# A fused attention and token-mixing kernel on one core: a new order of all units, with other evicting engines, PSUM banks and load order

## The chip, the cores and the metric

The kernel runs on one core of one Trainium2 chip. The metric is the device time of one execution in microseconds (us); smaller is better. Three timed runs of the kernel before gave 109.33, 109.36 and 109.76, median 109.36.

## What is computed

There are two parts, one behind the other. B = 4 batches, H = 8 heads, S = 768 positions, D = 64 values per head, 8 blocks of 96 positions.

```python
P = sort_net                                   # 8x8 per batch and head
for _ in range(5):                             # Sinkhorn: rows, then columns
    P = exp(P - max(P, -1)); P /= sum(P, -1); P /= sum(P, -2)
k_sorted = einsum('bhij,bhjcd->bhicd', P, k_blocks)      # mix whole blocks
v_sorted = einsum('bhij,bhjcd->bhicd', P, v_blocks)
attn = softmax(q_blocks @ k_sorted^T / 8)      # inside each block of 96
x = (attn @ v_sorted)  -> (B, S, 512)          # heads side by side
W = (x @ w_q) @ (x @ w_k)^T / 8
out = relu(W @ x) @ w_out
```

The inputs q, k, v are float32 in DRAM and are cast to bfloat16 by the load; the output is float32.

## The kernel before, in words

**Units.** The whole program is cut into small units, and a string, `ORDER` (L17 to L47), lists them one by one. The loop at L597 reads the list and calls one function per unit, which appends its instructions to its engine's queue. Nothing is scheduled by a tool: each engine runs its own units in just the order in which the string names them, and the framework adds a wait wherever a unit needs what another has written, or where a buffer or bank must first be read out. A unit's name is a kind, the batch and a number. An upper-case kind (other than R) is TensorE work, and the number after the colon is the PSUM bank that it writes. A lower-case kind is the eviction of that bank or other elementwise work, with the engine (A = ScalarE, called ACT; D = VectorE, called DVE; G = GpSimd, called POOL; S = SyncE, called SP) and the bank. So `K01:4 ... k01:A:4` is: unit K of batch 0, pair of heads 1, into banks 4 and 5; ACT evicts them.

The kinds, for a batch b:

- `lq`, `lk`, `lv` (L205): the load of q, k or v of one batch, 768 KB as bfloat16, issued by POOL; three buffers for each of the three inputs (`NIN`, L105). `lp` loads w_q and w_k, `lo` loads w_out.
- `i`, `c`, `a`, `p`, `B`, `u`, `n` (L158 to L241): constants; the Sinkhorn chain on DVE and ACT (`c00 a01 c01 ... a05 c05`); then its result laid out as mixing matrices `M` (unit `n`; for batch 0 on DVE from PSUM, for the others on POOL from the copy `PTR`).
- `Q`, `q` (L248): q transposed to `QT`. `K`, `k` (L269): k mixed by `M` and transposed in one step to `KT`, two banks.
- for batch 0 `Y`, `y`, `F`, `f` (L275 to L288): v mixed like k, then transposed back to `VT`. For the other batches `V`, `v` (L290): v mixed into the single buffer `Vs`, and six DMAs `R` on SP (L300), which move `Vs` row by row to `VT`.
- `S`, `e` (L304, L314): seven units of scores (S06, S16, ... are short) and their exponential on ACT, into `E`.
- `P`, `r`, `x` (L325 to L347): five units of attention times v (P04, P14, ... are short), reciprocal of the sums and product on DVE, into `X`.
- `T`, `t` (L350): X transposed to `XT`. `J`, `j`, `d`: the w_q and w_k product. `W`, `w`, `G`, `g`, `H`, `h`: the mixing, ending in `mixT` with the ReLU. `O`, `o`, `s`: six units of the last product, evicted to `ot` and stored by SP.
- `Z` (L243): filler. `Z09` multiplies a tile of zeros nine times and nobody reads it.

**Shared places.** PSUM has eight banks; a unit that writes a bank waits for the eviction of what stood there. `M`, `QT`, `KT`, `VT`, `E`, `X` have two buffers, `Vs` has one. POOL issues the loads one after the other between its `n` and `d` units, so a load stands behind whatever POOL waits for.

Of the kernel before, what the change touches and what calls it, by code (L numbers as in the profile page):

```python
# [14 lines left out]
NMIX = 2  # L15

ORDER = """  # L17
i02:D Z03:0 lq0 c00:D lk0 a01:A c01:D i00:G i03:G B01:0 p01:A a02:A p00:A:0 c02:D lq1 lv0 a03:A c03:D lv1
Z010:0 lk1 a04:A c04:D lp a05:A c05:D lk2 Q03:0 lq2 Q02:1 q03:A:0 Q01:2 B00:3 lo q01:D:2 q02:A:1 Q00:0 n03:D:3
lv2 n01:D:3 K03:1 n02:D:3 K01:4 q00:D:0 k03:A:1 lq3 K02:6 n00:D:3 k01:A:4 k02:D:6 S05:0 u00:A:3 S02:4 e05:A:0  # L20
S03:6 n10:G S04:2 e02:A:4 Q13:0 Q11:1 n11:G q13:D:0 e03:A:6 K00:4 q11:D:1 Q10:0 k00:A:4 S06:6 lk3 Q12:1
e06:A:6 S00:4 q12:D:1 q10:A:0 S01:6 e01:A:6 Y03:0 y03:A:0 e04:A:2 Y01:6 Y00:0 y01:D:6 y00:A:0 n20:G F03:3
Z09:2 f03:A:3 e00:A:4 F01:0 F00:1 f01:D:0 V12:2 f00:D:1 Y02:4 v12:A:2 P04:6 n21:G P01:0 r04:D:6 y02:A:4
x04:D:6 P00:2 R15:S r01:D:0 R14:S lv3 K13:4 r00:D:2 x01:D:0 K11:6 k13:A:4 k11:D:6 K10:0 S16:4 x00:D:2 e16:A:4
V11:6 V10:4 v11:A:6 k10:D:0 T00:3 n30:G F02:2 v10:A:4 t00:D:3 R13:S S11:0 f02:D:2 K12:6 R12:S e11:A:0 S10:4
n31:G k12:D:6 R10:S P02:2 e10:A:4 P03:0 R11:S r02:D:2 x02:D:2 S13:6 K20:4 e13:A:6 r03:D:0 T01:2 x03:D:0
k20:A:4 S14:6 t01:D:2 e14:A:6 T03:0 K22:3 t03:A:0 K23:1 k22:D:3 S15:6 T02:5 e15:A:6 k23:D:1 Q23:4 Q20:3
q23:A:4 Q22:6 t02:D:5 q20:D:3 q22:A:6 S12:0 P13:6 e12:A:0 J00:5 r13:D:6 x13:D:6 P10:3 j00:A:5 S24:0 d00:G
W00:5 r10:D:3 e24:A:0 P14:6 x10:D:3 J01:2 S20:0 j01:D:2 S25:3 e20:A:0 r14:D:6 w00:D:5 d01:G W01:2 x14:D:6
Q21:5 e25:A:3 P11:0 q21:D:5 S26:6 w01:D:2 T13:5 r11:D:0 e26:A:6 x11:D:0 V22:2 t13:A:5 V21:6 v22:A:2 P12:4  # L30
v21:D:6 V20:0 T10:2 R24:S r12:D:4 G00:3 v20:D:0 t10:A:2 R23:S K21:6 R22:S G01:3 k21:A:6 x12:D:4 R21:S Q31:0
g00:A:3 Q33:1 R20:S q31:D:0 H00:2 S21:4 R25:S q33:D:1 H02:6 h00:A:2 T11:0 h02:D:6 e21:A:4 T12:1 S22:2 t12:D:1
H01:6 t11:A:0 S23:4 h01:D:6 O00:1 e22:A:2 J11:0 o00:A:1 e23:A:4 K32:6 j11:D:0 K31:1 k32:D:6 d11:G J10:3
k31:D:1 K33:4 j10:A:3 K30:6 W10:3 d10:D k30:A:6 O02:0 k33:D:4 w10:A:3 W11:7 o02:A:0 S36:5 S35:3 w11:D:7 S32:1
e36:A:5 G10:7 e35:A:3 P22:5 e32:A:1 G11:7 r22:D:5 x22:D:5 V32:3 P23:0 v32:A:3 O05:2 g10:D:7 r23:D:0 x23:D:0
R35:S H11:6 o05:A:2 H10:4 R34:S Q30:3 h11:A:6 h10:D:4 T22:0 V30:1 q30:A:3 P24:6 t22:D:0 O11:5 v30:A:1 r24:D:6
x24:D:6 S30:3 o11:D:5 Q32:0 R31:S e30:A:3 P21:6 R30:S P20:1 q32:A:0 r21:D:6 V31:3 x21:D:6 T23:5 v31:A:3 O03:0
r20:D:1 t23:D:5 x20:D:1 S34:6 R32:S o03:A:0 S33:4 T21:3 R33:S e33:A:4 O04:0 t21:D:3 s01:S e34:A:6 S31:1
o04:D:0 H12:3 T20:5 e31:A:1 h12:D:3 O10:6 s02:S P32:0 o10:D:6 P33:2 r32:D:0 O01:4 s10:S r33:D:2 x32:D:0 O15:6
x33:D:2 P34:0 o15:A:6 O14:7 t20:D:5 P31:2 o01:D:4 o14:A:7 J20:5 r31:D:2 s00:S r34:D:0 x34:D:0 J21:4 s12:S  # L40
j20:A:5 x31:D:2 T32:7 d20:G j21:A:4 W20:0 T33:1 d21:G W21:6 w20:D:0 T31:2 t33:D:1 w21:A:6 G20:0 t31:D:2 P30:5
t32:D:7 G21:0 r30:D:5 x30:D:5 O12:7 g20:A:0 H21:0 o12:A:7 H20:2 H22:4 h21:D:0 h20:A:2 T30:6 O13:7 t30:D:6
O22:3 h22:D:4 o13:A:7 J30:2 s11:S o22:A:3 J31:7 j30:D:2 O21:6 d30:D j31:A:7 d31:D W30:7 W31:5 o21:A:6 O23:4
w31:D:5 w30:A:7 G30:7 o23:A:4 O24:6 s21:S G31:7 o24:A:6 O20:4 g30:A:7 H32:6 o20:D:4 H31:1 h32:A:6 O25:5
h31:D:1 s20:S H30:3 o25:A:5 O35:7 h30:D:3 s22:S O34:6 o35:D:7 O31:5 o34:A:6 s35:S O32:7 s34:S o31:A:5 O30:6
s31:S o32:A:7 O33:5 s32:S o30:A:6 s30:S o33:A:5 s33:S
"""  # L47


# [595 lines left out]
```

## Time and profile before

| what | value |
|---|---|
| median of 3 runs | 109.36 us |
| the profiled execution's own time | 109.27 us |
| its span (first to last instruction or transfer) | 107.4 us |
| TensorE (PE) matmul busy | 91.2 us, 85% |
| DVE busy | 72.3 us, 67% |
| ACT busy | 68.8 us, 64% |
| POOL busy | 28.4 us, 26% |
| loads, queue of POOL | 10.09 MB |
| stores and R transfers, queue of SP | 8.73 MB |

The span is 1.87 us shorter than the execution that it was taken from. "Busy" is time in which at least one instruction of the engine ran; for PE the ends of matmuls are modelled. PEld is the loading of weights, which goes on beside PE's matmuls. "PEclk" is the share of the full TensorE clock that was granted. In the lists of instructions a row has the start in us, the duration in us, the engine, the line, the operation, the tile written and the tiles read, a count (x24: so many merged into the row), and in brackets how long the engine stood idle before it and what ended that. Nearly all matmuls have line 143 and all copies line 147 (ACT) or 149 (DVE), since helpers issue them; they are told apart by their tiles.

### The profile page before, as it was taken

To read this page: it belongs to the slowest core of one execution; us is meant where nothing else is said; L and a number is where in the kernel's file an instruction comes from. 1 tells how busy PE (TensorE), PEld (TensorE's weight loads), DVE (VectorE), ACT (ScalarE), POOL (GpSimd) and SP (SyncE) were. 2 spreads that over 40 slices of the span, in tenths; PEclk is the share of its full clock that TensorE was granted. 3 is DMA by queue.
4 is the path that set the end of the run, shared out by engine and by line. 5 is a ranking of instruction groups with operands and counts; after the bars stand their busy time and mean duration, and the time that the engine had idled before them with its cause. 6 is when DMAs were issued, how large, how long until landed. Compare 5 with 4: busy or idle time off the path is not lost.

```text
span 107.4 us, 3466 instructions
## 1 busy us (share of the span) xinstructions
PE 91.2 (85%) x1475; PEld 61.4 (57%) x1486; DVE 72.3 (67%) x143; ACT 68.8 (64%) x99; POOL 28.4 (26%) x47
## 2 busy tenths in 40 slices
PE   5399477559889979599998999999999999999950
PEld 1135456453778868468985766785657755543410
DVE  3676963230479988399998858979899987219200
ACT  4404399796176998669789697989625174635550
POOL 6999122125897700011000100000001273000000
PEclk9999999985999999999999999999999999999999
DMA  0999999999999999999999400323974503145982
GB/s 3 100 198 205 203 205 205 203 204 205 186 204 215 228 233 243 205 205 203 207 209 263 85 6 0 101 55 96 359 279 166 240 0 148 50 198 206 362 310 98
DMA packets 18879, 19.04 MB, mean 177 GB/s; under 512 B 1840, under 2 KB 16944, under 8 KB 18864
## 3 DMA queue, kind: packets, MB, share of 16 engines
q0 software_dynamic: 14064, 10.09, 62.4%
q1 hardware_dynamic: 4800, 8.73, 23.5%
q8 instruction: 11, 0.18, 0.7%
q14 instruction: 4, 0.03, 0.1%
HBM read 20.19 MB, written 6.29 MB: 247 GB/s over the span
## 4 chain that ended last, share of the span: by engine, by line
PE 43%; DMA 24%; DVE 15%; POOL 8%; issue 4%; ACT 3%; DVEq 0%; SPq 0%; POOLq 0%; ACTq 0%
PE ps L143 43%; DMA Vn<-in_v_dram 17%; DMA VT<-Vs 7%; DVE X L344 6%; POOL M L239 2%; DVE mixT L410 2%; POOL Qn L215 2%; DVE Rall L339 1%; DVE Vs L149 1%; ACT Vs L147 1%; ACT E L315 1%; DVE ot L149 1%; POOL Kn L215 1%; DVE KT L149 1%; POOL Vn L215 1%
## 5 line engine op out<-in xcount | busy, mean ns | idle before, releaser
L315 ACT ACTIVATE E<-ps 96x960 bf16<-96x960 f32 (+1 forms) x28 | 24.4, 902 | 2.3 <-PE ps L143 2.1
L143 PE MATMUL ps<-wo,mixT 128*128 128x512 bf16 x86 | 22.4, 379 | 0.5
L344 DVE TENSOR_TENSOR X<-ps,Rall 96x896 bf16<-96x896 f32 (+1 forms) x20 | 19.8, 1000 | 0.4
L147 ACT COPY ot<-ps 128x512 f32<-128x512 f32 x18 | 10.6, 586 | 10.2 <-PE ps L143 10.1
L371 POOL COPY qD<-qkT 64x384 bf16<-64x384 bf16 x5 | 2.5, 503 | 43.9 <-ACT qkT L147 31.2
L143 PEld LDWEIGHTS <-mixT 128*128 128x128 bf16 x96 | 8.3, 98 | 8.6 <-issue 1.0
L143 PE MATMUL ps<-VT,E 96*128 96x65 bf16 x256 | 10.5, 193 | 1.3 <-DMA VT<-Vs 1.2
L149 DVE CAST KT<-ps 128x768 bf16<-128x768 f32 x10 | 9.4, 952 | 2.8 <-PE ps L143 2.8
L143 PEld LDWEIGHTS <-E 96*128 96x128 bf16 x256 | 9.3, 97 | 2.9 <-issue 1.7
L143 PE MATMUL ps<-fil 128*128 128x512 bf16 x21 | 9.1, 607 | 2.0 <-DVE fil L191 1.2
L143 PEld LDWEIGHTS <-KT 64*128 64x128 bf16 (+1 forms) x288 | 8.5, 98 | 4.1 <-issue 1.9
L147 ACT CAST KT<-ps 128x768 bf16<-128x768 f32 x10 | 7.9, 798 | 3.8 <-PE ps L143 3.7
L410 DVE TENSOR_SCALAR mixT<-ps 128x1024 bf16<-128x1024 f32 x8 | 9.8, 1222 | 0.5 <-PE ps L143 0.4
L147 ACT CAST Vs<-ps 128x1024 bf16<-128x1024 f32 x7 | 7.0, 1019 | 4.3 <-PE ps L143 3.8
L143 PE MATMUL ps<-QT,KT 64*128 64x96 bf16 x256 | 9.1, 204 | 0.5 <-ACT KT L147 0.5
L143 PE MATMUL ps<-idb,X 96*128 96x96 bf16 x128 | 8.0, 207 | 0.6 <-DVE X L344 0.6
L143 PE MATMUL ps<-idb,Qn 128*64 128x128 bf16 x192 | 7.5, 225 | 1.0 <-DMA Qn<-in_q_dram 0.9
L239 POOL TENSOR_TENSOR M<-PTR,m_p 128x512 bf16<-128x512 bf16 x6 | 7.8, 1310 | 1.3 <-PE ps L143 1.3
L143 PE MATMUL ps<-M,Kn 128*64 128x128 bf16 x192 | 7.2, 221 | 0.8 <-DVE X L344 0.4
L143 PEld LDWEIGHTS <-Qn 128*64 128x64 bf16 x192 | 6.2, 113 | 2.6 <-DMA Qn<-in_q_dram 1.9
L143 PEld LDWEIGHTS <-X 96*128 96x128 bf16 x128 | 6.2, 98 | 2.2 <-issue 0.6
L339 DVE RECIPROCAL Rall<-ps 96x14 f32<-96x14 f32 (+1 forms) x20 | 4.3, 223 | 4.7 <-PE ps L143 4.6
(79 smaller groups left out, 131.8 us busy)
## 6 DMA issues: line engine op xcount, KB each, us to landing
out_dram<-ot SPq DMA_DIRECT2D x9, 512.0 KB, 2.8
Qn<-in_q_dram POOLq DMA_DIRECT2D x4, 768.0 KB, 18.5
Kn<-in_k_dram POOLq DMA_DIRECT2D x4, 768.0 KB, 22.2
Vn<-in_v_dram POOLq DMA_DIRECT2D x4, 768.0 KB, 21.8
VT<-Vs SPq DMA_DIRECT2D x18, 132.0 KB, 5.8
out_dram<-ot SPq DMA_DIRECT2D x6, 256.0 KB, 2.0
wo<-in_moe_w_out_dram POOLq DMA_DIRECT2D x1, 512.0 KB, 25.1
wqk<-in_moe_w_q_dram POOLq DMA_DIRECT2D x1, 64.0 KB, 20.6
```

Source lines behind the costliest of these rows:

```text
L143: nc.tensor.matmul(o, w, x, is_transpose=t, start=start, stop=stop, skip_group_check=True)
L147: nc.scalar.copy(o, i)
L149: nc.vector.tensor_copy(o, i)
L215: nc.gpsimd.dma_start(out=t[b % NIN][:, h0:h1].rearrange("p h r d -> p h (r d)"), in_=src[b, h0:h1].rearrange("h (p r) d -> p h (r d)", p=P))
L239: ENG[e].tensor_tensor(out=M[b % 2][:, h0:h0 + hn], in0=src.unsqueeze(2).to_broadcast([P, hn, SP, NB]), in1=m_p.unsqueeze(1).unsqueeze(3). ...
L315: nc.scalar.activation(E[b % 2][:, n, 0:2 * w * BLK].rearrange("p (t a c) -> p a t c", a=2, c=BLK), PS[0:BLK, bank:bank + 2, 0:w * BLK].re ...
L339: nc.vector.reciprocal(Rall[:, b, n, :, 0:w], avps(bank, w)[:, :, :, D])
L344: nc.vector.tensor_mul(xo.rearrange("p (a t d) -> p a t d", a=2, d=D), avps(bank, w)[:, :, :, 0:D], Rall[:, b, n, :, 0:w].unsqueeze(3).to_ ...
L371: nc.gpsimd.tensor_copy(o, i)
L410: nc.vector.tensor_relu(o, i)
```

## The change

Only the string `ORDER` is changed. It holds the same work units; every engine's sequence, many evicting engines, the banks and the loads' places differ. Its first part, and the places of later parts that matter below:

```diff
 ORDER = """
-i02:D Z03:0 lq0 c00:D lk0 a01:A c01:D i00:G i03:G B01:0 p01:A a02:A p00:A:0 c02:D lq1 lv0 a03:A c03:D lv1
-Z010:0 lk1 a04:A c04:D lp a05:A c05:D lk2 Q03:0 lq2 Q02:1 q03:A:0 Q01:2 B00:3 lo q01:D:2 q02:A:1 Q00:0 n03:D:3
-lv2 n01:D:3 K03:1 n02:D:3 K01:4 q00:D:0 k03:A:1 lq3 K02:6 n00:D:3 k01:A:4 k02:D:6 S05:0 u00:A:3 S02:4 e05:A:0
-S03:6 n10:G S04:2 e02:A:4 Q13:0 Q11:1 n11:G q13:D:0 e03:A:6 K00:4 q11:D:1 Q10:0 k00:A:4 S06:6 lk3 Q12:1
-e06:A:6 S00:4 q12:D:1 q10:A:0 S01:6 e01:A:6 Y03:0 y03:A:0 e04:A:2 Y01:6 Y00:0 y01:D:6 y00:A:0 n20:G F03:3
-Z09:2 f03:A:3 e00:A:4 F01:0 F00:1 f01:D:0 V12:2 f00:D:1 Y02:4 v12:A:2 P04:6 n21:G P01:0 r04:D:6 y02:A:4
-x04:D:6 P00:2 R15:S r01:D:0 R14:S lv3 K13:4 r00:D:2 x01:D:0 K11:6 k13:A:4 k11:D:6 K10:0 S16:4 x00:D:2 e16:A:4
-V11:6 V10:4 v11:A:6 k10:D:0 T00:3 n30:G F02:2 v10:A:4 t00:D:3 R13:S S11:0 f02:D:2 K12:6 R12:S e11:A:0 S10:4
...
+i00:G i02:D lq1 B01:0 Z014:7 lv0 c00:D a01:A p01:A c01:D lq0 p00:A:0 lk0 a02:A c02:D i03:G lv1 a03:A c03:D lk1
+Z03:7 a04:A lk2 Q12:7 c04:D Q13:0 Q11:1 q13:A:0 Q10:2 Z03:3 a05:A q11:A:1 c05:D q12:D:7 B00:1 n01:D:1 n00:D:1
+Y01:6 n03:D:1 n02:D:1 y01:A:6 Y03:3 u00:D:1 Y00:5 n10:G y03:D:3 Y02:0 n11:G y02:A:0 Q02:3 y00:A:5 Q03:7
+q02:D:3 Q00:0 q03:D:7 F02:1 q00:D:0 F03:3 Q01:7 f03:D:3 q10:D:2 q01:D:7 K01:2 f02:D:1 K03:6 k01:A:2 K00:4
+k03:D:6 K02:0 n20:G k00:A:4 S02:2 k02:D:0 S05:6 e02:A:2 lq2 S03:0 e05:A:6 S01:2 S04:4 n21:G e04:A:4 F00:6
+F01:7 f00:D:6 e01:A:2 V12:4 f01:D:7 e03:A:0 P03:2 r03:D:2 v12:A:4 P02:0 x03:D:2 V11:6 S06:4 r02:D:0 V10:2
+e06:A:4 x02:D:0 v11:A:6 K10:4 k10:D:4 K11:0 v10:A:2 S00:6 k11:D:0 K12:4 e00:A:6 R10:S K13:2 R15:S P01:0 n31:G
+k12:A:4 P04:6 R12:S r01:D:0 k13:A:2 r04:D:6 S13:4 x01:D:0 R11:S lp e13:A:4 T02:2 R13:S x04:D:6 K22:0 t02:A:2
+R14:S S11:3 k22:D:0 lv2 T01:7 e11:A:3 T03:6 S12:0 n30:G t03:D:6 S16:2 e12:A:0 P00:4 t01:D:7 S15:6 r00:D:4 lq3
+e16:A:2 x00:D:4 K21:0 e15:A:6 Q21:2 Q22:3 lo k21:D:0 S14:4 T00:7 e14:A:4 q21:D:2 Q23:6 S10:0 t00:D:7 q23:A:6
+K23:4 q22:D:3 Q20:7 e10:A:0 k23:D:4 S23:2 J00:6 e23:A:2 q20:D:7 S24:0 j00:D:6 P12:4 e24:A:0 P11:2 r12:D:4
+V21:6 x12:D:4 W00:0 J01:1 v21:A:6 r11:D:2 w00:D:0 V22:4 x11:D:2 j01:A:1 R23:S V20:6 v22:A:4 d01:G W01:0
...
+q32:D:6 Z03:7 t10:D:0 h01:A:2 P14:6 q33:D:1 O05:0 r14:D:6 x14:D:6 T12:2 o05:D:0 S20:3 S21:5 t12:D:2 T11:7
+e21:A:5 T13:0 t11:D:7 O02:2 e20:A:3 t13:D:0 S26:6 H00:0 o02:D:2 e26:A:6 J10:5 h00:A:0 K31:6 j10:D:5 K30:2
...
```

- **Loads.** Before: q0, k0, q1, v0, v1, k1, w_q and w_k, k2, q2, w_out, v2, q3, k3, v3. Now: q1, v0, q0, k0, v1, k1, k2, q2, w_q and w_k, v2, q3, w_out, k3, v3. On POOL the identity matrix (`i00`) now stands ahead of the first load, `n10`, `n11` and `n20` ahead of q2, `n31` ahead of w_q and v2, and `d01` ahead of k3.
- **Start.** Before: q of batch 0, its k and its scores and exponentials, then v. Now: q of batch 1, v of batch 0 (`Y`, later `F`), q of batch 0, and only then k and the scores of batch 0.
- **Fillers.** 22 filler multiplications before (3, 10, 9), 23 now (14, 3, 3 near the start, 3 among batch 1's T and P units).
- **Evictions.** From ACT to DVE: 4 more of q, 7 more of the last product `o`, and one each of `f`, `j` and `u`; from DVE to ACT: 4 of the ReLU `h` and one each of `k` or `y`, `v` and `w`.

More of the change, by code (lines that the diff above doesn't have):

```diff
@@ L23 @@
-Z09:2 f03:A:3 e00:A:4 F01:0 F00:1 f01:D:0 V12:2 f00:D:1 Y02:4 v12:A:2 P04:6 n21:G P01:0 r04:D:6 y02:A:4
-x04:D:6 P00:2 R15:S r01:D:0 R14:S lv3 K13:4 r00:D:2 x01:D:0 K11:6 k13:A:4 k11:D:6 K10:0 S16:4 x00:D:2 e16:A:4
-V11:6 V10:4 v11:A:6 k10:D:0 T00:3 n30:G F02:2 v10:A:4 t00:D:3 R13:S S11:0 f02:D:2 K12:6 R12:S e11:A:0 S10:4
-n31:G k12:D:6 R10:S P02:2 e10:A:4 P03:0 R11:S r02:D:2 x02:D:2 S13:6 K20:4 e13:A:6 r03:D:0 T01:2 x03:D:0
-k20:A:4 S14:6 t01:D:2 e14:A:6 T03:0 K22:3 t03:A:0 K23:1 k22:D:3 S15:6 T02:5 e15:A:6 k23:D:1 Q23:4 Q20:3
@@ L28 @@
[L28 to L46, printed above, removed]
+i00:G i02:D lq1 B01:0 Z014:7 lv0 c00:D a01:A p01:A c01:D lq0 p00:A:0 lk0 a02:A c02:D i03:G lv1 a03:A c03:D lk1
+Z03:7 a04:A lk2 Q12:7 c04:D Q13:0 Q11:1 q13:A:0 Q10:2 Z03:3 a05:A q11:A:1 c05:D q12:D:7 B00:1 n01:D:1 n00:D:1
@@ new lines @@
+v20:D:6 G00:1 lk3 w01:A:0 P13:2 P10:4 lv3 r13:D:2 R21:S S22:6 x13:D:2 G01:1 R20:S e22:A:6 d00:G Q30:0 R22:S
+r10:D:4 K20:2 x10:D:4 g00:A:1 R25:S Q31:7 k20:A:2 Q33:1 R24:S Q32:6 q30:D:0 H02:4 q31:D:7 H01:2 h02:A:4 T10:0
+q32:D:6 Z03:7 t10:D:0 h01:A:2 P14:6 q33:D:1 O05:0 r14:D:6 x14:D:6 T12:2 o05:D:0 S20:3 S21:5 t12:D:2 T11:7
+e21:A:5 T13:0 t11:D:7 O02:2 e20:A:3 t13:D:0 S26:6 H00:0 o02:D:2 e26:A:6 J10:5 h00:A:0 K31:6 j10:D:5 K30:2
+k31:A:6 K32:0 d10:G K33:4 k32:D:0 k30:A:2 W10:6 J11:7 k33:A:4 P20:0 S25:2 r20:D:0 w10:D:6 P21:4 e25:A:2
@@ new lines @@
+x20:D:0 O00:6 j11:A:7 r21:D:4 P23:2 x21:D:4 o00:A:6 V31:0 O01:7 v31:A:0 r23:D:2 d11:D x23:D:2 V32:5 T20:4
+R33:S v32:A:5 V30:0 t20:D:4 R32:S P22:2 o01:D:7 v30:A:0 W11:4 R34:S G10:5 w11:D:4 r22:D:2 S34:6 x22:D:2 R31:S
+S33:0 e34:A:6 G11:5 R35:S O03:4 g10:D:5 e33:A:0 s00:S R30:S H11:5 S36:2 H10:0 h11:D:5 e36:A:2 O04:7 h10:A:0
+o03:D:4 S30:2 S35:5 e30:A:2 P24:0 o04:D:7 s01:S O11:4 r24:D:0 e35:A:5 s02:S x24:D:0 T21:7 S32:2 o11:A:4
+t21:D:7 H12:0 S31:5 e32:A:2 h12:D:0 O10:7 e31:A:5 P34:2 T23:4 r34:D:2 P32:0 o10:A:7 x34:D:2 P31:5 t23:A:4
@@ new lines @@
+s10:S r32:D:0 T22:7 r31:D:5 P30:2 x32:D:0 t22:A:7 O14:4 r30:D:2 P33:0 x30:D:2 o14:A:4 J20:7 x31:D:5 J21:4
+j20:A:7 O12:2 r33:D:0 d20:D j21:D:4 W20:7 T30:5 d21:G w20:D:7 W21:4 o12:D:2 O15:6 w21:A:4 x33:D:0 T31:4
+o15:A:6 G20:7 t31:D:4 s12:S T32:0 T33:6 t32:A:0 G21:7 t33:D:6 O13:4 t30:D:5 g20:A:7 H22:6 o13:A:4 H20:0 H21:2
+h22:D:6 h20:A:0 J31:5 s11:S J30:4 h21:A:2 j31:D:5 O21:0 d31:G j30:A:4 W31:1 d30:D O20:7 w31:A:1 W30:1 O22:6
+w30:A:1 o21:A:0 G30:1 o22:D:6 O23:0 o20:D:7 G31:1 s20:S o23:A:0 O24:7 g30:A:1 s21:S H30:0 o24:D:7 H32:5
@@ L47 @@
+h30:A:0 O25:4 h32:A:5 H31:2 o25:D:4 O31:0 h31:D:2 s22:S O30:7 o31:A:0 O34:5 s31:S o30:D:7 O33:0 s30:S o34:D:5
+O32:7 s34:S o33:D:0 O35:5 s33:S o32:A:7 s32:S o35:A:5 s35:S
 """
```

## The prediction, made before the changed kernel was run

> **What bounds the kernel now.** I read the page's totals first, then the busy time of each engine in five stretches.
>
> ```profile
> PE 91.2 (85%) x1475; PEld 61.4 (57%) x1486; DVE 72.3 (67%) x143; ACT 68.8 (64%) x99; POOL 28.4 (26%) x47
> ```
>
> ```profile
> 0.00:20.90 20.90, 13.71 (x237) 8.15 (x237) 12.34 (x47) 11.87 (x20) 11.33 (x25) 1.00 1.10 164
> 20.90:33.20 12.30, 10.19 (x165) 7.44 (x167) 5.33 (x10) 6.85 (x9) 8.45 (x8) 0.86 1.39 200
> 33.20:58.41 25.21, 22.79 (x507) 18.78 (x508) 22.43 (x35) 21.18 (x27) 3.90 (x5) 1.00 1.27 221
> 58.41:103.41 45.00, 44.51 (x568) 27.05 (x575) 32.24 (x53) 28.31 (x44) 4.75 (x10) 1.00 0.43 153
> 103.41:107.40 3.99, 0.00 (x0) 0.00 (x0) 0.00 (x0) 0.59 (x1) 0.00 (x0) 1.00 0.45 173
> ```
>
> The columns are the stretch and its length, then busy us of PE, PEld, DVE, ACT, POOL, the granted clock, the DMA share and GB/s. From 58.41 on PE is busy for 44.51 of 45.00 us: that stretch is bound by PE's work, and only less of it left at 58.41 shortens it. From 33.20 to 58.41 PE (22.79), DVE (22.43) and ACT (21.18) are all near 25.21; nothing there has much slack. The first 20.9 us wait for loads, as the weight loads' idle times on PE show; the last row shows POOL, which has waited for the fifth:
>
> ```profile
> 9.29 1.26 PEld L143 LDWEIGHTS <-Qn 128*64 128x64 bf16 x36 [0.84 <-DMA Qn<-in_q_dram]
> 12.93 1.03 PEld L143 LDWEIGHTS <-Kn 128*64 128x64 bf16 x36 [0.39 <-DMA Kn<-in_k_dram]
> 16.78 0.70 PEld L143 LDWEIGHTS <-Qn 128*64 128x64 bf16 x24 [1.06 <-DMA Qn<-in_q_dram]
> 20.91 0.75 PEld L143 LDWEIGHTS <-Vn 128*64 128x64 bf16 x25 [1.32 <-DMA Vn<-in_v_dram]
> 25.31 0.88 POOL L215 DMA_DIRECT2D Qn<-in_q_dram  x1 [3.28 <-DMA Vn<-in_v_dram]
> ```
>
> The first four loads land at about 9.3, 12.9, 16.8 and 20.9, and the fifth by 25.3: 3.9 us apiece, whatever they hold.
>
> **The change, part by part.** PE's real work is the same; so I ask how much of it is done at one time in both, and what is different behind it.
>
> *Loads ahead.* The first four are now q1, v0, q0, k0. All of batch 0 is there after the fourth, as before. `i00` on POOL now stands before the first issue:
>
> ```profile
> 1.27 1.13 POOL L215 DMA_DIRECT2D Qn<-in_q_dram  x1 [0.82 <-POOLq L629]
> ...
> 3.28 0.22 POOL L186 MEMSET idb<- 128x128 bf16 x1
> 3.58 0.35 POOL L187 TENSOR_SCALAR_AFFINE_SELECT idb<-idb 128x128 bf16<-128x128 bf16 x1
> ```
>
> It ends 0.65 us after it starts (3.28 to 3.93); part may fall in the 0.82 us that POOL idles now. Bounds 0 and 0.65; I take 0.4, so k0 lands at 21.3. Until then PE has Q1, Y0, Q0 and half of F0, 14 units of under 0.5, and time to spare. The end of the Sinkhorn chain, which Y0 needs, moves too: `a05` now stands behind `q13` on ACT.
>
> ```profile
> 9.86 0.26 ACT L159 ACTIVATE Pm<-Pm 32x64 f32<-32x64 f32 x1 [1.50 <-DVE Pm L180]
> ...
> 11.62 0.23 DVE L182 STREAM_TRANSPOSE PbT<-Pb 32x64 bf16<-32x64 bf16 x1
> ```
>
> From `a05` to the end of the chain is 2.0 us (9.86 to 11.85). `q13` ends near 11.3 (9.3 + 0.4, two Q units, one copy of 0.8), so the chain ends near 13.3, and with the four `n` Y0 near 16: still ahead of q0 at 17.2. All this hides behind the loads.
>
> *From k0 to P04.* Now every exponential of batch 0 comes after k0, on one engine in one sequence: k01, k00, e02, e05, e04, e01, e03, v12, e06, v11, v10, e00.
>
> ```profile
> L315 ACT ACTIVATE E<-ps 96x960 bf16<-96x960 f32 x24 | 22.5, 971 | 1.6 <-PE ps L143 1.5
> ...
> L147 ACT CAST KT<-ps 128x768 bf16<-128x768 f32 x10 | 7.9, 798 | 3.8 <-PE ps L143 3.7
> ...
> L147 ACT CAST Vs<-ps 128x1024 bf16<-128x1024 f32 x7 | 7.0, 1019 | 4.3 <-PE ps L143 3.8 <-ACT E L315 0.4
> ...
> L315 ACT ACTIVATE E<-ps 96x384 bf16<-96x384 f32 x4 | 2.0, 488 | 0.7 <-PE ps L143 0.6
> ```
>
> 2 x 0.80 + 6 x 0.97 + 0.49 + 3 x 1.02 = 10.97 us. It starts when K01 is done, 21.3 + 0.43, so `e00` ends at 32.7 without a gap; following banks and evictions by hand I find about 0.5 us of gaps (v12 waits for bank 4, e06 for S06), so P04, whose bank 6 `e00` reads out, starts at 33.2. PE's own work there, some 9.3 us, fits in. The sixth load, k1 (28.7 by the spacing, +0.4), is there before K10 at about 30.2.
>
> At 33.2 the kernel before starts V11 and has P04, P01 and P00 behind it. The changed one has V11, V10, K12, F02 and one full P more, and S16 and P04 less. So the next stretch is, before, V11 to J11 (33.2 to 58.41), and in the changed kernel P04 to J10. Counting units, the changed one has there 2 Q, one O and three fillers more; 2 V, one K and one F less, and one S and one P short instead of full. With these rows:
>
> ```profile
> 53.90 0.86 PE L143 MATMUL ps<-idb,Qn 128*64 128x128 bf16 x24
> ...
> 58.41 0.81 PE L143 MATMUL ps<-XT,wqk 128*128 128x384 bf16 x4
> ```
>
> ```profile
> 70.86 1.04 PE L143 MATMUL ps<-VT,E 96*128 96x65 bf16 x28
> ...
> 73.49 0.60 PE L143 MATMUL ps<-QT,KT 64*128 64x96 bf16 x20
> ```
>
> ```profile
> 98.05 5.35 PE L143 MATMUL ps<-wo,mixT 128*128 128x512 bf16 x23
> ```
>
> ```profile
> 33.20 1.05 PE L143 MATMUL ps<-Vn,M 128*128 128x128 bf16 x16
> ```
>
> (the J row marks the end of the stretch) a Q, or a K of the same shape, is 0.43, a P 0.52, an S 0.30, an O 4 x 5.35/23 = 0.9, a V or F (eight matmuls) about 0.5, three fillers at the pace of O 0.7. Sum: 0.86 + 0.9 + 0.7 - 1.0 - 0.43 - 0.5 - 0.15 - 0.2 = +0.2 us. So that stretch has the same PE work. Behind it the changed kernel has one O and two Q less and one S more than the kernel before behind J11: -0.9 - 0.86 + 0.3 = **-1.5 us**. Lead: 1.3 us.
>
> *What DVE and ACT carry.* I multiplied the units of the middle stretch by the means of their groups; the larger ones of DVE are
>
> ```profile
> L344 DVE TENSOR_TENSOR X<-ps,Rall 96x896 bf16<-96x896 f32 x16 | 17.2, 1079 | 0.3
> ...
> L410 DVE TENSOR_SCALAR mixT<-ps 128x1024 bf16<-128x1024 f32 x8 | 9.8, 1222 | 0.5 <-PE ps L143 0.4
> L149 DVE CAST KT<-ps 128x768 bf16<-128x768 f32 x10 | 9.4, 952 | 2.8 <-PE ps L143 2.8
> ...
> L149 DVE COPY XT<-ps 128x768 bf16<-128x768 bf16 x12 | 6.5, 544 | 0.2 <-PE ps L143 0.2
> ...
> L149 DVE COPY QT<-ps 128x768 bf16<-128x768 bf16 x9 | 4.7, 545 | 3.2 <-PE ps L143 3.1
> ...
> L149 DVE COPY ot<-ps 128x512 f32<-128x512 f32 x6 | 4.1, 685 | 3.9 <-PE ps L143 3.9
> ...
> L149 DVE CAST Vs<-ps 128x1024 bf16<-128x1024 f32 x2 | 2.4, 1192 | 0.1
> ```
>
> Before, 6 large products and a short one, 4 K, 2 V, 2 h, 4 T, 4 q and small ones give 23.5 us; after, 6 and 2 short, 3 K, 1 V, 2 o, 7 T, 7 q and small ones give 23.5 as well. ACT falls from 22.5 to 20.2. Behind the stretch ACT has 31.1 (30.3 before) and DVE 32.0 (34.0), both far below PE's 43. So the changed kernel is no more engine-bound than this one, and I give it the same pace.
>
> *R transfers.* Before, PE waits for the last of them:
>
> ```profile
> 44.44 0.53 PE L143 MATMUL ps<-VT,E 96*128 96x65 bf16 x12 [1.23 <-DMA VT<-Vs]
> ```
>
> ```profile
> L301 SPq DMA_DIRECT2D VT<-Vs x18: 546/598/1452, 30.4 to 74.0; - x18
> ```
>
> ```profile
> 36.75 7.55 DMA VT<-Vs
> ```
>
> Now all six follow `v10`, which ends near 32.2; six issues of 0.6 (the second row's median) end by 35.9, and with the 7.55 us that the last one takes now (third row, of the chain of work) they are there at 43.4 at the latest. P12, their first reader, has 9.2 us of PE work and 10.2 us of DVE work between it and P04, so it comes at 42.4 to 43.6. The wait shrinks from 1.2 to between 0 and 1; I take a gain of 1.2 less 0.2.
>
> *What is late next.* v2 is read by V21, just behind P12. Its issue now stands behind `n31`, which needs the last K of batch 1 (32.7):
>
> ```profile
> 13.17 0.88 POOL L215 DMA_DIRECT2D Qn<-in_q_dram  x1 [2.34 <-DMA Kn<-in_k_dram]
> ...
> Qn<-in_q_dram POOLq DMA_DIRECT2D x1, 768.0 KB, 25.2
> ```
>
> The eighth load, here q2, lands at 13.17 + 25.2 = 38.4; w_q, w_k and v2 behind it need 0.7 + 4 to 4.5, so 43.3 to 44. V21 is due at 43.4 to 44.6. I charge 0.3 us. q3, w_out, k3 and v3 have 1 to 3 us of slack by the same count. The last six O units and their stores end as they do now, so the 3.99 us behind PE's end stay.
>
> **The sum.** Lead 1.3, R wait 1.0, v2 -0.3: PE ends at 103.4 - 2.0 = 101.4, the span is 105.4. The execution takes 1.87 us more than its span: 109.27 - 2.0 = **107.3 us**. The median of the runs shown is 0.09 above that execution.
>
> **A rule on the clock.** The trace has one stretch at half clock, and what went before it is this:
>
> ```profile
> 20.44:23.85 3.41, 2.05 (x44) 1.89 (x46) 0.96 (x1) 2.74 (x4) 0.89 (x1) 0.94 1.32 205
> 23.85:27.27 3.42, 3.20 (x11) 1.29 (x10) 0.00 (x0) 1.88 (x2) 1.94 (x2) 0.56 1.33 202
> ```
>
> PE was busy 2.05 of 3.41 us, and the next 3.4 us ran at 0.56; nine fillers filled them. The changed order has only six fillers between 9 and 50 us and sparse PE work between 13 and 30. A half-clock stretch there doubles up to 1.7 us of work; where ACT leads it costs 0.4, where PE leads all 1.7. The Trainium skill (TensorE: Matmul & The Clock Gate, Part 1) says that the clock halves after an idle window of about 3.4 us. By that rule no gap that I foresee is long enough and nothing is lost; by this trace, a window 60% busy was enough, so the row speaks for the rival.
>
> **The rivals.**
>
> 1. *Half clock in the head*: +0.4 to +1.7, so 107.7 to 109.0. For it: the row above. Against: from 9 to 17 PE is as sparse in the trace before and stays at 1.00. Chance 0.15.
> 2. *The lead is used up*: VT, v2 or the tight middle stretch takes 1.4 to 2.6 us, since DVE and PE each have over 23 us in 24: 108.7 to 109.9. Chance 0.20. For it: every queue is new, and PE, DVE and ACT wait on each other there. Against: the kernel before runs the same sums in 25.2.
> 3. *ACT's head chain breaks up* (slower): the 10.97 us of evictions after k0 depend on five K, S, V and P banks in turn. If ACT is full for only 75% (it is 6.85 of 12.30 in this stretch before), the chain takes 14.6 us instead of 11.5 and P04 comes 3.1 late: 110.4. It decides from 13.5 us on (full under 81%), where the 2.0 is gone; 14.0 is slower by over 0.5%. Against: where exponentials queue in the trace they run back to back. Chance 0.17.
> 4. *Nothing is late, VT and v2 are early*: another 0.5 to 1.5 us, 105.8 to 106.8. Chance 0.08.
>
> **How the numbers follow.** The forecast, 106.8 to 107.9, has 0.40. Faster by over 0.5% is under 108.8 (that is about what a measurement of this kernel can tell from no change): 0.40, 0.08, most of rival 1 (0.13) give 0.61. Within 0.5%: the rest of rival 1 and most of rival 2, 0.20. Slower: rival 3 and the end of rival 2, 0.19. The range leaves out 0.05 below and, above, the worse half of rival 3: 105.8 to 110.4.
>
> **What the changed profile would show.** K01's weights waiting for DMA until 21.0 to 21.6 (the 0 to 0.65 of `i00`); ACT without gaps until `e00`, and P04 near 33.2 (12 us after k0: forecast; 15: rival 3); PEclk under 0.9 in a slice between 13 and 30, or later (rival 1); PE's waits for VT and Vn near 43.5, and J10 at about 57.5 to 58 (later than 59.5: rival 2). I am wrong altogether if PE idles much behind J10, where I see no reason for it.

## The result, and the profile after

The changed kernel takes 107.0 us (median of four executions, 106.2 to 108.29), the kernel before on the same chip 109.34. The ratio is 0.975 with a 95% interval of 0.971 to 0.979: 2.1 to 3.0% faster. Here and below medians are over all executions, and ratios leave out slow ones (here 108.29; of graft 1 below three of six, the other three took 111.61 to 112.05). The profiled execution took 106.73 us with a span of 104.9, 2.5 us less than the span before.

This is the busy time of the engines in the stretches that answer to those of the prediction (columns as there): up to the landing of k0, to P04, to J10, to PE's last work, and the tail.

```profile
0.00:21.30 21.30, 14.57 (x195) 9.30 (x196) 14.31 (x51) 6.80 (x13) 10.72 (x23) 0.92 1.08 162
21.30:32.99 11.69, 9.69 (x246) 8.50 (x247) 7.48 (x11) 10.45 (x13) 3.91 (x4) 1.00 1.32 204
32.99:57.00 24.01, 22.43 (x491) 17.70 (x490) 21.66 (x38) 18.76 (x25) 8.98 (x11) 1.00 1.28 212
57.00:100.92 43.92, 42.88 (x553) 26.50 (x558) 30.94 (x52) 28.92 (x42) 4.75 (x10) 1.00 0.51 168
100.92:104.90 3.98, 0.00 (x0) 0.00 (x0) 0.00 (x0) 0.59 (x1) 0.00 (x0) 1.00 0.48 187
```

Beside the stretches of the kernel before the ends move like this: +0.4 at the landing (21.30 against 20.90), -0.2 at P04 against V11 (32.99, 33.20), -1.4 at J10 against J11 (57.00, 58.41), -2.5 at PE's end (100.92, 103.41). The middle stretch gave 1.2 us, the one behind it 1.1, in which PE is busy 1.6 us less (the O and the two Q units that are already done) and idle half a microsecond more. ACT is busy 10.45 of 11.69 us between the landing and P04, where it was 6.85 of 12.30: the head chain that the prediction wrote down.

These are rows of PE in the changed kernel, with the wait for k0, the end of P01 and P04 (one row of 22 matmuls, the last eight of them P04, from about 33.0), and V21's wait for v2:

```profile
21.30 1.53 PE L143 MATMUL ps<-M,Kn 128*64 128x128 bf16 x48 [1.77 <-DMA Kn<-in_k_dram]
...
32.45 0.84 PE L143 MATMUL ps<-VT,E 96*128 96x65 bf16 x22
...
44.67 0.62 PE L143 MATMUL ps<-Vn,M 128*128 128x128 bf16 x8 [0.29 <-DMA Vn<-in_v_dram]
...
57.00 0.82 PE L143 MATMUL ps<-XT,wqk 128*128 128x384 bf16 x4
```

The prediction had 21.3 for k0, 33.2 for P04, 0.3 us for v2, and about 57.5 to 58 for J10.

### The profile page after: what moved, and what is told of

The parts are those of the page before. It is cut to its first block, busy times and chain, and to the rows that moved or that the text cites. A ratio compares the mean times of both kernels' runs of the same rounds, so it can differ in the third digit from the quotient of the medians.

```text
span 104.9 us, 3468 instructions
## 1 busy us (share of the span) xinstructions
PE 89.6 (85%) x1477; PEld 62.0 (59%) x1487; DVE 74.4 (71%) x150; ACT 65.5 (62%) x92; POOL 28.4 (27%) x47
## 4 chain that ended last, share of the span: by engine, by line
PE 43%; DMA 33%; POOL 6%; DVE 4%; ACT 4%; SPq 3%; issue 3%; POOLq 0%; ACTq 0%; DVEq 0%
PE ps L143 43%; DMA Kn<-in_k_dram 16%; DMA Vn<-in_v_dram 9%; DMA VT<-Vs 8%; ACT E L315 3%; SPq L301 3%; DVE KT L149 3%; POOL Qn L215 2%; POOL wqk L208 1%; POOL M L239 1%; DVE X L344 1%; POOL Vn L215 1%; DVE Rall L339 1%; ACT ot L147 1%; POOL idb L187 0%
## 5 line engine op out<-in xcount | busy, mean ns | idle before, releaser
L143 PE MATMUL ps<-wo,mixT 128*128 128x512 bf16 x88 | 23.3, 380 | 0.5 <-issue 0.2
L149 DVE COPY ot<-ps 128x512 f32<-128x512 f32 x13 | 8.8, 686 | 5.3 <-PE ps L143 5.1
L147 ACT COPY ot<-ps 128x512 f32<-128x512 f32 x11 | 6.5, 588 | 6.8 <-PE ps L143 4.6
L149 DVE CAST KT<-ps 128x768 bf16<-128x768 f32 x9 | 8.4, 954 | 2.8 <-PE ps L143 2.7
L147 ACT CAST Vs<-ps 128x1024 bf16<-128x1024 f32 x8 | 7.9, 1014 | 1.6 <-PE ps L143 1.2
L408 ACT ACTIVATE mixT<-ps 128x1024 bf16<-128x1024 f32 x8 | 7.8, 1018 | 1.5 <-PE ps L143 1.5
L143 PE MATMUL ps<-idb,Qn 128*64 128x128 bf16 x192 | 6.9, 221 | 1.5 <-DMA Qn<-in_q_dram 1.5
L143 PEld LDWEIGHTS <-Kn 128*64 128x64 bf16 x192 | 5.8, 109 | 3.5 <-DMA Kn<-in_k_dram 2.4
L143 PE MATMUL ps<-fil 128*128 128x512 bf16 x21 | 7.7, 522 | 0.2 <-issue 0.2
L149 DVE COPY QT<-ps 128x768 bf16<-128x768 bf16 x13 | 6.7, 543 | 1.2 <-PE ps L143 1.2
## 6 DMA issues: line engine op xcount, KB each, us to landing
Qn<-in_q_dram POOLq DMA_DIRECT2D x4, 768.0 KB, 12.1
```

The costliest lines, as they stand in the source:

```text
L143: nc.tensor.matmul(o, w, x, is_transpose=t, start=start, stop=stop, skip_group_check=True)
L147: nc.scalar.copy(o, i)
L149: nc.vector.tensor_copy(o, i)
L408: nc.scalar.activation(o, i, ACT.Relu)
```

## Experiments

**Two theories at first.** Theory 1, the prediction's: the gain is PE work that is done earlier in the head, plus the shorter wait for the R transfers. Theory 2: the gain comes from behind the head, from the new evicting engines, banks and order. Four grafts were to tell them apart: one kernel's order up to a cut, and then all that is left in the other's order. Each grafted list differs from its first kernel from the cut on; where a bank was still in use at the joint, a free one was taken.

Graft 1, the kernel before up to V11:

```diff
 K10:0 S16:4 x00:D:2 e16:A:4
-V11:6 V10:4 v11:A:6 k10:D:0 T00:3 n30:G F02:2 v10:A:4
+F02:6 f02:D:6 P03:2 r03:D:2 P02:4 x03:D:2 V11:6 r02:D:4
...
```

> The units of the kernel before up to V11 (33.2 us in its trace), then all that is left in the order, banks and evicting engines of the changed kernel; its middle filler of 3 is kept. Theory 1 (the gain is the amount of PE work done by 33 us, plus the R wait): no lead, so PE's end moves by +0.65 for the filler and between 0 and -1.2 for the R wait: 108.4 to 109.9. Theory 2 (the gain comes from the new evicting engines, banks and order behind the head): 107.0 to 107.6. A clumsy joint can add up to 0.5.

Graft 2, the changed kernel up to P04:

```diff
 R15:S P01:0 n31:G k12:A:4
-P04:6 R12:S r01:D:0 k13:A:2 r04:D:6 S13:4 x01:D:0
+lp lo lv2 lq3 lk3 P04:6 r04:D:6 x04:D:6 P00:4 r01:D:0
...
```

> The units of the changed kernel up to P04, then all that is left in the order, banks and evicting engines of the kernel before. Theory 1: the lead at 33 us is V11, V10, K12, F02 and a full P more, S16 and P04 less, about 1.9 us of PE work, with P04 at 32.9 instead of 33.2, and no middle filler: 106.5 to 107.5. Theory 2: 108.8 to 109.6.

Graft 3, the changed kernel up to J10:

```diff
 S26:6 H00:0 o02:D:2 e26:A:6
-J10:5 h00:A:0 K31:6 j10:D:5 K30:2 k31:A:6 K32:0
+S25:3 e25:A:3 h00:A:0 O00:1 J11:0 o00:A:1 K32:6
...
```

> The units of the changed kernel up to J10 (57.0 us in its trace), then all that is left in the order of the kernel before. Theory 1: all of the gain is there by J10, and the rest runs at PE's pace in either order: 106.5 to 107.5. Theory 2 (a better late part, with ACT relieved of 7 evictions of the last product): 108 to 109.5.

Graft 4, the kernel before up to J11:

```diff
 S23:4 h01:D:6 O00:1 e22:A:2
-J11:0 o00:A:1 e23:A:4 K32:6 j11:D:0 K31:1 k32:D:6
+e23:A:4 Q30:0 Q32:6 q30:D:0 q32:D:6 O05:0 o05:D:0
...
```

> The units of the kernel before up to J11 (58.41 us in its trace), then all that is left in the order of the changed kernel. Theory 1: 108.9 to 109.8. Theory 2: 107 to 108.2.

Measured: 112.82, 111.96, 112.24 and 111.14 us, with ratios of 1.019 (1.012 to 1.026), 1.021 (1.015 to 1.028), 1.019 (1.010 to 1.029) and 1.014 (1.009 to 1.020). All four are slower than both kernels, as neither theory had it. The list of what PE waited for in graft 3 (in all, times, longest) shows one reason, and the stretches behind the joints of grafts 2 and 3 another:

```profile
PE ps L143 <- ACT mixT L408: 2.0, 1, 2.0
```

```profile
33.00:45.00 12.00, 7.88 (x146) 6.39 (x142) 6.00 (x10) 7.19 (x10) 8.00 (x9) 0.72 1.33 216
```

```profile
58.00:70.00 12.00, 9.60 (x146) 6.43 (x148) 5.61 (x10) 6.51 (x10) 0.50 (x1) 0.86 0.34 54
```

In graft 3 `h00` now stands behind `e25` on ACT, and O00 right behind it waits 2.0 us, a wait that neither kernel has. In graft 2 PE waits 2.0 us for a product and 1.6 us for an exponential right behind the joint. And where both kernels have the full clock, it is 0.72 of it in graft 2 from 33 to 45 us and 0.86 in graft 3 from 58 to 70. So in these two the joint itself brings waits as long as the difference that it was to place, and half clock on top: the grafts are inconclusive on the two theories.

**The evicting engines alone.** Order, banks and loads stay those of the kernel before; 55 evictions take the engine that they have in the changed kernel. The first seven of them, without the units between:

```diff
-q03:A:0 q02:A:1 k03:A:1 u00:A:3 q13:D:0 q11:D:1 q10:A:0
+q03:D:0 q02:D:1 k03:D:1 u00:D:3 q13:A:0 q11:A:1 q10:D:0
...
```

> The order, banks and loads of the kernel before, with the evicting engines of the changed kernel (55 evictions change sides). If the new evicting engines alone made the gain (theory 2): 106.8 to 108. If they only go with the new order (theory 1, where the balance of the engines is the same in both): 109.3 to 112, slower since the alternation of ACT and DVE around each unit is broken.

Measured: 114.77 us, ratio 1.046 (1.042 to 1.050). That is more than either theory had. The new engines by themselves are no gain; put on the old order they cost 5 us, and why so much was not taken apart. Theory 2 falls as far as it rests on them.

**The load order alone.** The changed kernel, with the old sequence of loads at the places of the new ones (the loads alone, without the units between):

```diff
-lq1 lv0 lq0 lk0 lv1 lk1 lk2 lq2 lp lv2 lq3 lo lk3 lv3
+lq0 lk0 lq1 lv0 lv1 lk1 lp lk2 lq2 lo lv2 lq3 lk3 lv3
```

> The changed kernel with the loads issued in the order of the kernel before (q0, k0, q1, v0, v1, k1, w_q and w_k, k2, q2, w_out, v2, q3, k3, v3), at the places where the changed one issues loads. All theories: PE's queue begins with Q1 and Y0, which then wait until 16.8 and 20.9; K01 comes behind Y0, Q0 and F0 near 25 instead of 21.3, so 3 to 4 us more: 110 to 111. If it were under 108, the load order would be no part of the change that matters.

Measured: 118.9 us, ratio 1.084 (1.081 to 1.088): the sign is right, the size is far off, 12 us over the changed kernel instead of 4. PE's rows show why, with the two stretches at half clock behind them (in this list and in most below, the helpers' lines are one lower, since `ORDER` has a line less):

```profile
16.52 2.77 PE L142 MATMUL ps<-idb,Qn 128*64 128x128 bf16 x48 [9.28 <-DMA Qn<-in_q_dram]
...
28.47 1.53 PE L142 MATMUL ps<-M,Kn 128*64 128x128 bf16 x48 [0.79 <-DVE QT L148]
...
50.12 1.49 PE L142 MATMUL ps<-idb,Qn 128*64 128x128 bf16 x24 [4.68 <-DMA Qn<-in_q_dram]
```

```profile
12.10:25.75 13.65, 8.20 (x133) 7.20 (x136) 5.15 (x15) 3.55 (x6) 2.55 (x2) 0.50 1.32 205
49.65:56.47 6.82, 6.35 (x100) 5.10 (x101) 2.98 (x5) 2.90 (x4) 0.00 (x0) 0.50 1.30 205
```

K01 comes at 28.47, 7.2 us after the changed kernel's and 3.5 later than expected. Y0 also waits for a Sinkhorn chain that waits for `q13`, and starts at 21.8. The second reason is the clock, which no expectation had: PE has stood idle for 9.28 us, and all its work from 12.1 to 25.8 runs at half clock (Y0's 48 matmuls take 2.81 us there, 2.05 at full clock in the kernel without the middle filler). The old sequence also puts q2 where the issue stands behind `n31` on POOL, at 41.0; PE waits 4.68 us for it, and half clock follows once more: from Q2 to J00 it is 5.9 us instead of the changed kernel's 4.2. Order of units, order of loads and what POOL does between the loads go together.

**The R wait.** In the kernel before, J00 is moved ahead of P13, which waits 1.2 us for the last R transfer:

```diff
-S12:0 P13:6 e12:A:0 J00:5 r13:D:6 x13:D:6 P10:3 j00:A:5
+S12:0 J00:5 P13:6 e12:A:0 r13:D:6 x13:D:6 P10:3 j00:A:5
```

> The kernel before with one unit moved: J00 ahead of P13, so that it fills the 1.2 us for which PE waits for the last R transfer. Theory 1 (that wait is on the path): 0.6 to 0.75 less, 108.6 to 108.8. Rival (the products x13 and x10 behind P13 are what PE waits for next, so the wait costs nothing): 109.2 to 109.5.

Measured: 109.43 us, ratio 1.001 (0.998 to 1.005). The wait is filled in part and nothing is won:

```profile
44.63 1.03 PE L142 MATMUL ps<-VT,E 96*128 96x65 bf16 x28 [0.50 <-DMA VT<-Vs]
...
46.74 0.41 PE L142 MATMUL ps<-VT,E 96*128 96x65 bf16 x8 [0.41 <-DVE X L343]
...
58.55 0.81 PE L142 MATMUL ps<-XT,wqk 128*128 128x384 bf16 x4
```

Half a microsecond of the wait stays, another 0.41 us appears before P14 as a wait for the product on DVE, and J11 comes at 58.55 (58.41 before). So the 0.7 us of the wait that is filled is worth nothing in the old order, where the prediction had 1.0 us for this term; the half that stays was not tried.

**The middle filler.**

```diff
-H01:2 h02:A:4 T10:0 q32:D:6 Z03:7 t10:D:0 h01:A:2 P14:6
+H01:2 h02:A:4 T10:0 q32:D:6 t10:D:0 h01:A:2 P14:6
```

> The changed kernel without its middle filler (Z03 between H01 and T10). The prediction charged three fillers at warm pace, 0.65 us, as pure loss. Theory 1 (PE is the bound there): 0.5 to 0.65 less than the changed kernel, 106.1 to 106.5. Rival (PE waits for the product of x10 or for other evictions there, and the filler only fills the wait): no change, 106.8 to 107.2.

Measured: 106.36 us (105.58 to 107.02), ratio 0.969 (0.965 to 0.974). The time lies in the range of theory 1, but the interval overlaps that of the changed kernel, so the times don't decide. The traces do for the place of the filler. First the changed kernel from T10 on, then the one without the filler:

```profile
51.86 0.52 PE L143 MATMUL ps<-idb,X 96*128 96x96 bf16 x8
52.21 0.81 PE L143 MATMUL ps<-fil 128*128 128x512 bf16 x2
52.86 0.41 PE L143 MATMUL ps<-VT,E 96*128 96x65 bf16 x8
53.11 1.03 PE L143 MATMUL ps<-wo,mixT 128*128 128x512 bf16 x4
```

```profile
51.95 0.52 PE L142 MATMUL ps<-idb,X 96*128 96x96 bf16 x8
52.58 0.41 PE L142 MATMUL ps<-VT,E 96*128 96x65 bf16 x8
53.11 1.02 PE L142 MATMUL ps<-wo,mixT 128*128 128x512 bf16 x4
```

O05 starts at 53.11 and J10 at 57.00 in both. O05 writes bank 0, which T10 has just filled and `t10` on DVE must first read out (52.41 to 52.97 in the changed kernel). T10 itself is only 0.09 us earlier in the changed kernel. So the filler stands in that wait: the rival's reading holds, and the 0.7 us charged for it is not there. The traces part behind J10: there the changed kernel waits 0.4 us for an R transfer in front of batch 2's first P and the one without the filler does not, and PE ends 0.5 us earlier. Whether the filler has to do with that wait is not shown.

**More fillers in the head.**

```diff
-Q10:2 Z03:3 a05:A q11:A:1
+Q10:2 Z09:3 a05:A q11:A:1
...
-q01:D:7 K01:2 f02:D:1
+q01:D:7 Z06:5 K01:2 f02:D:1
```

(The middle filler is left out here too.)

> The changed kernel without the middle filler, and with 12 fillers more in two waits of PE in the head: six more before B00, where PE waits for the Sinkhorn chain, and six before K01, where it waits for k0. Theory 1 (PE's head is bound by loads and by ACT, a cold clock there costs little): as without the middle filler, 106.0 to 106.6. Rival (a half-clock stretch in the head costs up to 1 us in some executions): the median falls by 0.3 to 0.8 more and the executions lie closer together.

Measured: 107.28 us (106.71 to 111.56), ratio 0.978 (0.974 to 0.982). That is above both expectations: no gain and no closer spread; fillers in the head buy nothing. Why its median lies above that of the kernel without them stays open: its profiled execution, which is its fastest, has J10 at 56.90 and a span of 104.6.

**DVE relieved.** Without the middle filler, and

```diff
-W01:0 v20:D:6 G00:1
+W01:0 v20:A:6 G00:1
...
-P14:6 q33:D:1 O05:0
+P14:6 q33:A:1 O05:0
```

> The changed kernel without the middle filler, with two evictions moved from DVE to ACT: v20 and q33, 1.7 us of DVE between 47 and 54 us, where DVE runs back to back and ACT stands idle twice for 1.2 us. Theory 4 (DVE's sequence sets when T10 and O05 can run): O05 at 52.5 instead of 53.1, J10 at 56.4 instead of 57.0, 105.7 to 106.1. Rival (PE, or ACT's new wait, is the bound): J10 at 57.0, no change against 106.4 for the kernel without the filler alone.

Measured: 106.58 us, ratio 0.974 (0.970 to 0.978), as without the two moves. This is DVE around the place of v20, and PE's O05 and J10:

```profile
48.25 0.24 DVE L338 RECIPROCAL Rall<-ps 96x14 f32<-96x14 f32 x1 [1.51 <-PE ps L142]
...
52.24 0.56 DVE L148 COPY XT<-ps 128x768 bf16<-128x768 bf16 x1
```

```profile
51.15 0.28 PE L142 MATMUL ps<-qkT,Ab 64*128 64x256 bf16 x1
...
52.85 1.02 PE L142 MATMUL ps<-wo,mixT 128*128 128x512 bf16 x3
...
56.74 0.82 PE L142 MATMUL ps<-XT,wqk 128*128 128x384 bf16 x4
```

DVE now waits 1.51 us for PE in front of r13, and O05 still comes as soon as `t10` has run. The 0.26 us by which J10 is earlier are there in the H units already (51.15 against 51.40 without the moves). So theory 4's 0.6 us is not there. The rows read as if the one step T10, t10, O05 through one bank decided near 50 us, and not DVE's total; no run gave O05 another bank, so that is not shown.

**What held the kernel before.** Theory 1 says how much work is done by 33 us, not why the kernel before has less. Its chain of work says it, in lines that the prediction passed over:

```profile
6.68 18.09 DMA Vn<-in_v_dram
...
25.31 0.88 POOL Qn L215
26.19 0.01 issue
26.20 2.58 POOL M L239 x2
28.79 0.05 issue
28.83 1.22 PE ps L143 x24
```

These are PE's rows there, with the fillers, the second half of V12, and P04 at the head of the last row; then POOL's row for `n10` and `n11` in the changed kernel:

```profile
24.21 3.21 PE L143 MATMUL ps<-fil 128*128 128x512 bf16 x8 [0.22 <-issue]
...
28.83 0.40 PE L143 MATMUL ps<-Vn,M 128*128 128x128 bf16 x4 [0.30 <-POOL M L239]
...
29.62 1.31 PE L143 MATMUL ps<-VT,E 96*128 96x65 bf16 x36
```

```profile
15.18 2.57 POOL L239 TENSOR_TENSOR M<-PTR,m_p 128x512 bf16<-128x512 bf16 x2 [6.28 <-DVE PTR L149]
```

In the kernel before, POOL doesn't issue q3 before v1 has landed, at 24.8, and `n10` and `n11`, which need nothing but a copy made at 15, stand behind that issue. V12 waits for them until 28.83 and P04 stands behind V12. In the changed kernel the two run at 15.18. That is theory 3. First the two loads alone:

```diff
-n03:D:3 lv2 n01:D:3
+n03:D:3 n01:D:3
...
-q00:D:0 k03:A:1 lq3 K02:6
+q00:D:0 k03:A:1 K02:6
...
-Q13:0 Q11:1 n11:G q13:D:0
+Q13:0 Q11:1 n11:G lv2 lq3 q13:D:0
```

> The kernel before with two loads moved on POOL: lv2 and lq3 stand behind n10 and n11 instead of ahead of them. In its trace n10 starts only at 26.20, since POOL stands in front of q3's issue until v1 has landed, and V12 waits for n11 until 28.83. Theory 3 (part of the gain is that n10 and n11 no longer stand behind late loads): V12 comes when the fillers and F00 are through, 28.2 instead of 28.8: 0.3 to 0.7 less, 108.7 to 109.2. Theory 1 (the lead comes from the new order of units on PE and ACT): no change, 109.2 to 109.6.

Measured: 108.85 us, ratio 0.992 (0.989 to 0.995), as theory 3 had it. One of the nine executions had the full clock throughout and took 107.66; the others, at 0.96 to 0.98, took 108.58 to 109.51. Then without the nine fillers as well:

```diff
-Y00:0 y01:D:6 y00:A:0 n20:G F03:3 Z09:2 f03:A:3
+Y00:0 y01:D:6 y00:A:0 n20:G F03:3 f03:A:3
```

> The same, and the nine fillers at 24.2 us are left out. Theory 3: F01, F00 and V12 run at 24.3 to 25.5, P04 at about 26.5 instead of 29.6, and K13 when k1 lands, near 29 instead of 31.0; some 2 us of lead, 107.0 to 107.8, as fast as the changed kernel, whose order of units would then be no part of the gain. Theory 1: what is won at 30 us is lost again before 58 us, 108.6 to 109.5; a cold clock can take 0.3 to 1 us of it.

Measured: **107.39 us**, ratio 0.983 (0.979 to 0.987), again as theory 3 had it. These are PE's rows for the first P, K13 and J11, first of the loads moved alone, then with the fillers left out:

```profile
28.68 1.31 PE L142 MATMUL ps<-VT,E 96*128 96x65 bf16 x36
30.09 0.86 PE L142 MATMUL ps<-M,Kn 128*64 128x128 bf16 x24
...
57.72 0.81 PE L142 MATMUL ps<-XT,wqk 128*128 128x384 bf16 x4
```

```profile
23.34 2.72 PE L142 MATMUL ps<-idb,KT 128*96 128x128 bf16 x24 [0.34 <-ACT E L314]
...
27.30 1.30 PE L142 MATMUL ps<-VT,E 96*128 96x65 bf16 x36
28.84 0.86 PE L142 MATMUL ps<-M,Kn 128*64 128x128 bf16 x24 [0.24 <-DMA Kn<-in_k_dram]
...
56.59 0.81 PE L142 MATMUL ps<-XT,wqk 128*128 128x384 bf16 x4
```

P04 moves from 29.6 to 28.7 and 27.3; K13 from 31.0 to 30.1 and 28.8, where it now waits for k1; J11 from 58.41 to 57.72 and 56.59; the span from 107.4 to 106.7 and 105.6. What is won at 30 us is there at 58 us and at the end. P04 was expected at 26.5; the 24 matmuls of the F units in front of it run at half clock (0.50 from 23.4 to 26.8) and take 2.72 us, where 16 of them take 1.05 at full clock in the changed kernel. Two small edits of the old order bring 2.1 us (109.51 to 107.39 on one chip), about as much as the whole new order (2.3 us). The fillers were not left out alone; by the rows above V12 would still wait for `n11` until 28.83.

## Why the prediction was right

- *k0 at 21.3*: 21.30, by luck. `i00` ahead of the loads cost 0.19 us at the first issue (1.46 instead of 1.27), and q0, the third load, is there when it was before (Q0 at 16.82; the third load was read at 16.78). The 0.4 us comes at the fourth load alone, for a reason that no run shows; in the kernel with the two moves K01 starts at 21.08.
- *ACT's chain, P04 at 33.2*: 33.0. The chain is there and nearly full. Of the two gaps foreseen the one in front of e06 came and the one in front of v12 did not; the second is in front of e00:

```profile
29.01 0.49 ACT L315 ACTIVATE E<-ps 96x384 bf16<-96x384 f32 x1 [0.43 <-PE ps L143]
...
31.56 0.97 ACT L315 ACTIVATE E<-ps 96x960 bf16<-96x960 f32 x1 [0.24 <-PE ps L143]
```

So `e00` ended at 32.5. P04 began half a microsecond later, behind P01 and without a wait: at its very end PE's own work set the time, not the chain.

- *The lead in PE work*: right in kind. -1.5 us was forecast behind J10. PE is busy 1.6 us less there, but idle 1.0 us instead of 0.5, 0.4 of it for an R transfer, so the stretch is 1.1 shorter.
- *The middle stretch*: the forecast had it 0.5 us shorter (+0.2 of work, -1.0 for the R wait, +0.3 for v2); it is 1.2 shorter. Two terms are wrong singly. Of the R wait 0.7 us were filled in the old order and won nothing (109.43 against 109.51), and the filler, 0.7 counted in the +0.2, costs at most 0.1 in its place. v2's 0.29 us was right. By the stretches' rows PE is busy 0.4 us less (22.43, 22.79) and idle 0.8 us less. Why it idles less is not settled: DVE has 21.66 us of work there and had 22.43 (the prediction gave it 23.5 in both), but taking 1.7 us off DVE won nothing.
- *The sum*: 107.3 against 107.0 (106.73 for the profiled execution). The errors of its terms, -0.2 at P04, -0.7 in the middle and +0.4 behind it, partly cancel; that the sum is nearer than its terms is luck.
- *The cause*: the prediction counted the lead and did not ask why the kernel before lacked it. The experiment with two edits shows that POOL's `n10` and `n11` behind a late issue, and nine fillers, held the kernel before. So the new order is one way to that lead, not the only one. That the changed kernel gains by the same is read from its trace (`n10` and `n11` at 15.18, V12 at 26.04) and not shown: no run took this alone out of it. The new order seems to add something of its own: on one chip the kernel with the two moves, which has the new order, took 106.58 (0.970 to 0.978) and the old order with the two edits 107.39 (0.979 to 0.987). What that is, no run isolates.
- *The clock rival*: the half-clock stretch came, and cost nothing that the trace shows. These are the stretches ahead of it and its own, cut where the granted clock changes, in the kernel before and in the changed one:

```profile
20.05:23.46 3.41, 1.66 (x41) 1.50 (x42) 0.96 (x1) 2.76 (x4) 0.89 (x1) 1.00 1.31 205
23.46:26.87 3.41, 3.19 (x14) 1.49 (x13) 0.00 (x0) 2.24 (x3) 1.54 (x2) 0.50 1.32 203
```

```profile
10.11:13.53 3.42, 1.53 (x32) 0.99 (x28) 2.20 (x9) 1.57 (x3) 0.00 (x0) 1.00 1.32 204
13.53:16.94 3.41, 2.93 (x52) 2.69 (x53) 2.45 (x6) 1.15 (x2) 1.76 (x2) 0.50 1.31 203
```

The prediction cut its windows 0.4 us late, as their 0.94 and 0.56 tell: PE was busy for 1.66 us ahead of the fall, 49% and not 60%. Y0's 48 matmuls took 2.81 us, and 2.05 in the kernel without the middle filler, whose profiled execution has no such stretch; both end before q0 lands, near 16.7. The Trainium skill (TensorE: Matmul & The Clock Gate, Part 1) asks for an idle window of about 3.4 us. Here as in the kernel before, half-busy PE was enough, so this trace differs from the rule. That such a stretch comes and goes between executions (the kernel with the two moves had a mean clock of 0.976 to 1.000 in its six) agrees with the page, which calls the window free-running.

## What to carry to other kernels

When a list of units is ordered by hand, compare two orders by the work that the bound engine has done at one time, and then ask of the chain of work what held the slower one there; the answer can be two loads moved and one filler dropped where the change rewrites the whole list. Look at what stands behind a load's issue on the issuing engine: an issue that waits for an earlier load holds up the small operations behind it. A wait that ends last in one place is only worth its length if nothing else is due at the same time, and that is cheap to try: fill it with a unit from behind. Where a variant comes out far off its expectation, look at its granted clock before looking for other causes.

## What the runs showed of the hardware

POOL's issue of a load stood still until an earlier load had landed: in the kernel before for 2.34 us ahead of q2, and for about 3 us ahead of each of the next three, always ending with the landing of the load issued seven loads earlier (w_q and w_k counted as one). In the trace the landings of POOL's transfers are counted on eight semaphores in turn, and w_q and w_k are two transfers, so each wait is for the last use of the same semaphore. Whether POOL's queue or the program asks for that wait, no run shows.

Stretches of half clock of 3.41 us followed windows in which PE was busy for 1.66 us (before) and 1.53 us (changed). In the kernel without the middle filler a window with 1.61 us was followed by none, and in the changed kernel none followed the stretch from 16.94 on, in which PE did nothing but transposes (Q and F):

```profile
19.23:22.65 3.42, 1.61 (x56) 1.46 (x54) 2.44 (x5) 0.98 (x2) 0.27 (x1) 1.00 1.32 204
22.65:26.06 3.41, 2.62 (x71) 2.33 (x72) 1.65 (x3) 3.41 (x5) 3.24 (x3) 1.00 1.31 204
```

```profile
16.94:20.35 3.41, 2.59 (x64) 2.26 (x64) 2.72 (x6) 1.15 (x2) 0.81 (x1) 1.00 1.32 205
```

So PE's busy share alone does not tell when the clock falls.
